# Block transposes on VectorE and piecewise transfers in place of TensorE transposes, in a fused attention and ELU feed-forward kernel

## The chip, the cores and the metric

The kernel runs on one core of a Trainium2 chip. The metric is the device time of one execution in microseconds. The profile adds one traced execution, with the start, the duration and the releaser of every instruction.

## The reference

`x` is (8, 8, 512, 64): batch, head, token, depth. `state` is (8, 8, 32, 64). For each batch and head there are two small attentions, and their results are concatenated along the tokens and reshaped to 4352 rows of 512. These rows go through a feed-forward layer with an ELU between two products.

```python
scores = x @ state.T / 8               # 512 x 32 per head
xread  = softmax(scores) @ state
scores2 = state @ x.T / 8              # 32 x 512 per head
sread  = softmax(scores2) @ x
h   = concat(xread, sread) @ w_in      # 512 -> 2048
out = elu(h) @ w_out                   # 2048 -> 512
```

## The kernel before

**Stages.** The tokens of one batch (512 rows) are one unit of work. Batch 0 is interleaved by hand with the loading and conversion of the weights (`first_batch`, line 706); its written plan also computes the attention of batch 1. Then `batch(b)` (line 814) runs for b = 1 to 7. It has two parts: `ffn1` (line 412), sixteen column blocks `fo` of the first product, each followed by the ELU (`exp_part` on ScalarE, `max_part` on VectorE, into `g_all`); and the second product by Strassen's method (from line 531), where single products are themselves split once more (`Second`, line 472). At the end `states` (line 852) does the rows of the states of all batches.

**The attention of the next batch.** `batch(b)` puts the attention of batch b+1 into its second product. `attention` (line 668) returns a list of functions, `hooks`; after each step of the Strassen product one of them is called (lines 843 to 846). A full product is six half-size pieces p1a, p1b, p2a, p2b, p6a, p6b, and then the split products, in the order 7, 5, 4, 3; in batch 1 only 4 and 3 are split, and products 7 and 5 are two pieces each. Before the change the hooks are: `s0` after p1a, which turns `x` on TensorE (`turn_x`, line 225) into four PSUM banks and copies it out with ScalarE (`copy_x`); `s1` after p1b, with the scores (`scores`, line 261), the combined weights m = state @ w_in (`make_m`, line 377) and the chain of both softmaxes over VectorE, ScalarE and GpSimd; `s2` after p6a, which turns the states' softmax weights `a_s` on TensorE (`turn_state`, line 321), copies them out (`copy_state`, into `aT_s`) and turns the tokens' weights on VectorE (`turn_tokens`, `t_sb` to `aT`); and `state_read` (line 333) after p6b, the product of `aT_s` with `x`.

**Order.** Instructions issued through `InOrder` (line 93) keep the order in which the program calls them as long as `on` is true. For TensorE and for the transfer queue of SyncE it stays true. For VectorE it is true until the end of the `ffn1` loop of batch 1 (line 827) and false afterwards; for ScalarE and GpSimd it is false from batch 1 on. There a scheduler sets the order when the program is built. Since the helper at line 100 records every operation, the profile gives nearly all instructions line 100, and they are told apart by the names of their tiles.

**Buffers.** The pool `o` (line 76) has two buffers; before the change `xT` (the turned `x`) and the two output tiles `o_sb` share it. The pool `work` (tag `w`) has eleven; six of them hold the weight sums `t_w` for good, and five rotate over `s`, `s_2`, `aT_s` and others. `x_sb` has one buffer, so `load_x` of the next batch waits for `state_read`. `w_in` holds half of the first weight at a time: `fetch_w_in(2, 0)` and `fetch_w_in(0, 0)` bring the halves back from a copy in DRAM, two transfers of 1 MB each, on SyncE's queue.

**PSUM.** `ffn1` rotates over banks 3, 4 and 5. A split product accumulates into two banks, called x and y, seven times four matmuls (`Second.run`, line 505): x, y, x, y, x, y, x. After each four, VectorE adds a bank to `o_sb` or ScalarE copies it; the next four that go to the same bank wait for that.

Of the kernel before, what the change touches and what calls it, by code (L numbers as in the profile page):

```python
# [10 lines left out]
FP32 = mybir.dt.float32  # L11
# [14 lines left out]
def kernel(  # L26
# [15 lines left out]
    B, H, S, D = x.shape  # L42
    NS = state.shape[2]
    DM, DF = moe_w_in.shape
    P = 128
    R = S // P
    NP = H // 2
    G = 2
# [16 lines left out]
    def pool(name, bufs, **kw):  # L65
        return ctx.enter_context(tc.tile_pool(name=name, bufs=bufs, **kw))
# [6 lines left out]
    work = pool("work", NRAW + 4)  # L73
    small = pool("small", 4)
    epool = pool("elu", 3)
    opool = pool("o", 2)
# [8 lines left out]
    def bank(i):  # L85
        return psum[:, i]

    def pair(i):

        return psum[:, i : i + 2]  # L90
# [3 lines left out]
    class InOrder:  # L94
# [10 lines left out]
    tensor, sync, vector, scalar, gpsimd = (  # L105
        InOrder(e) for e in (nc.tensor, nc.sync, nc.vector, nc.scalar, nc.gpsimd)
    )
    matmul = tensor.matmul

    def transpose(out, in_):  # L110


        for t in range(2):
            rows = slice(t * 64, (t + 1) * 64)
            tensor.transpose(out[:, t], in_[rows], ident[rows, rows], tile_position=(t * 64, 0))
# [15 lines left out]
    x_t, st, m_t = {}, {}, {}  # L131

    def load_x(b, engines):
        x_t[b] = xpool.tile([P, R, DM], FP32, name="x_sb")
        x_v = x[b].rearrange("h (p r) d -> p r h d", r=R)
        for r in range(R):
            engines[r % len(engines)].dma_start(
                out=x_t[b][:, r].rearrange("p (h d) -> p h d", d=D), in_=x_v[:, r]
            )

    state_v = state.rearrange("b (m c) n d -> c m n b d", c=G)

# [82 lines left out]
    def turn_x(b, i, first=6):  # L225

        ps = pair(first).rearrange("p t (j r q) -> p t j r q", j=2, q=64)
        for j in range(2):
            for r in range(R):
                m = 2 * i + j  # L230
                transpose(ps[:, :, j, r], x_t[b][:, r, m * P : (m + 1) * P])
        st[b, "xT", i] = ps

    def copy_x(b, i):
        xT = opool.tile([P, 2, R * P], FP32, tag="o", name="xT")
        for j in range(2):
            st[b, 2 * i + j] = xT[:, j]
            scalar.copy(
                out=xT[:, j].rearrange("p (r t q) -> p t r q", t=2, q=64),
                in_=st[b, "xT", i][:, :, j],  # L240
            )
# [19 lines left out]
    def scores(b):  # L261

        st[b, "s_ps"] = by_state(b, [st[b, m][:, None] for m in range(NP)])
# [57 lines left out]
    def turn_state(b):  # L321
        ps = st[b, "sT"] = pair(6).rearrange("p g (r q) -> p g r q", r=R)
        for g in range(G):
            a = st[b, g, "a_s"].rearrange("p (r q) -> p r q", r=R)
            for r in range(R):
                tensor.transpose(ps[:, g, r], a[:, r], ident)

    def copy_state(b):
        st[b, "aT_s"] = work.tile([P, G, R, P], FP32, tag="w", name="aT_s")
        for g in range(G):  # L330
            scalar.copy(out=st[b, "aT_s"][:, g], in_=st[b, "sT"][:, g])

    def state_read(b):


        ps = st[b, "sr"] = pair(6)
        for g in range(G):
            for r in range(R):
                for m in range(NP):
                    matmul(  # L340
                        ps[m * NS : (m + 1) * NS, g, :D],
                        st[b, "aT_s"][:, g, r, m * NS : (m + 1) * NS],
                        x_t[b][:, r, m * P + g * D : m * P + (g + 1) * D],
                        start=(r == 0),
                        stop=(r == R - 1),
                        tile_position=(0, m * NS),
                    )

    def keep_read(b):
        for g in range(G):  # L350
            scalar.activation(
                out=read[:, b, g], in_=st[b, "sr"][:, g, :D], func=AF.Copy,
                scale=st[b, g, "total"],
            )
# [14 lines left out]
    def fetch_w_in(c, k):  # L369

        for i in range(2):
            sync.dma_start(
                out=w_in[:, 2 * (k + i) : 2 * (k + i) + 2],
                in_=w_in_mem[:, 2 * (c + i) : 2 * (c + i) + 2],
            )

    def make_m(b, c, h=None, first=6):

        c_in = c if b < 2 else c % 2
        halves = slice(2 * c_in, 2 * c_in + 2) if h is None else slice(2 * c_in + h, 2 * c_in + h + 1)  # L380
        assert h is None or b == 0
        st[b, "m", c] = by_state(b, [w_in[:, halves, m] for m in range(NP)], first)

    def copy_m(b, c, g, copy):
        if g == 0:
            m_t[b, c] = mpool.tile([P, G, 512], FP32, name="m_sb")
        copy(out=m_t[b, c][:, g], in_=st[b, "m", c][:, g])
# [8 lines left out]
    def exp_part(ps):  # L396
        e = epool.tile([P, ps.shape[-1]], FP32, tag="e", name="e_sb")
        scalar.activation(out=e, in_=ps, func=AF.Relu, scale=-1.0)
        scalar.activation(out=e, in_=e, func=AF.Exp, scale=-1.0)
        return e  # L400

    def max_part(fo, e, ps):
        vector.scalar_tensor_tensor(
            out=g_all[:, fo, : ps.shape[-1]], in0=e, scalar=-1.0, in1=ps,
            op0=ALU.add, op1=ALU.max,
        )

    def elu(ps, fo):

        max_part(fo, exp_part(ps), ps)  # L410

    def ffn1(b, fo):


        ps = bank(4 + fo % 2 if b == 0 else 3 + (fo + 1) % 3)
        for k in range(G):
            matmul(
                ps,
                m_t[b, fo // 4][:, k, fo % 4 * P : (fo % 4 + 1) * P],
                st[b, k, "aT"],  # L420
                start=(k == 0),
                stop=(k == G - 1),
            )
        return ps
# [243 lines left out]
    def attention(b):  # L668


        def both(*fs):
            for g in range(G):
                for f in fs:
                    f(b, g)

        def s0():

            for i in range(2):
                turn_x(b, i, 4 + 2 * i)
            for i in range(2):  # L680
                copy_x(b, i)

        def s1():

            scores(b)
            for c in range(2):
                make_m(b, c, first=4 - 2 * c)
            both(column_max, turn_scores, column_exp, row_max, row_subtract, row_exp)
            both(row_sum, row_scale, column_total)
            for c in range(2):  # L690
                for g in range(G):
                    copy_m(b, c, g, (scalar.copy, vector.tensor_copy)[g])

        def s2():
            turn_state(b)
            copy_state(b)
            both(turn_tokens)

        nop = lambda: None
        return [s0, s1, nop, nop, s2, lambda: (state_read(b), keep_read(b))]  # L700

    def store(b, i, o_sb):
        rows = out_b[b, 0:S].rearrange("(p r) c -> p r c", r=R)
# [108 lines left out]
            store(0, i, o_sb)  # L812

    def batch(b):
        for fo in range(FO):
            elu(ffn1(b, fo), fo)
            if fo == FO // 4 + 1:
                for c in (2, 3):
                    make_m(b, c, first=6 if c == 2 else 0)
            if FO // 4 + 1 <= fo < FO // 4 + 5:  # L820
                c, g = divmod(fo - FO // 4 - 1, G)
                copy_m(b, 2 + c, g, vector.tensor_copy)
            if b == 1 and fo % 2 == 1:
                weight_sum((1, 2, 4, 3)[fo // 4], fo % 4 // 2)
            if b > 1 and fo == FO // 4 + 2:
                fetch_w_in(0, 0)
        vector.on = False
        nxt = b + 1 < B
        hooks = attention(b + 1) if nxt else [turn_read]
        if nxt and b > 0:  # L830
            s1 = hooks[1]
            hooks[1] = lambda: (s1(), fetch_w_in(2, 0))
        if b + 2 < B:
            hooks += [lambda: load_x(b + 2, [sync])]
        if b == 1:
            hooks += [lambda: second[4].weights(t_w[4]), lambda: second[3].weights(b22)]
            hooks += [lambda: second[5].weights(t_w[1]), lambda: second[7].weights(t_w[3])]
            used = {k: second[k] for k in (4, 3)}
        else:
            used = second  # L840
        whole = Strassen(2, used)
        whole.sums()
        for f in whole.steps():
            f()
            if hooks:
                hooks.pop(0)()
        if not nxt:
            fetch_w_in(2, 2)
        for i in (1, 0):
            store(b, i, whole.o_sb[i])  # L850
# [28 lines left out]
    for b in range(1, B):  # L879
        batch(b)  # L880
# [31 lines left out]
```

## Time and profile before

| | |
|---|---|
| median of 3 runs | 756.91 us (756.82 to 757.55) |
| profiled span | 756.0 us |
| transposes of `x` on TensorE (64x64, in all) | 256, 11.8 us busy |
| transposes of `a_s` on TensorE (128x128, in all) | 64, 8.4 us busy |
| ScalarE copies `xT`, `aT_s` (all batches) | 16.6 us and 8.6 us busy |

In the table by groups a line gives engine, operation, output and inputs by tile name, shape, count, then busy time, mean duration of one, and the idle time of the engine just before them with what ended it. A timeline line gives start, duration, engine, operation and count. TensorE records two matmuls for each fp32 product and one for each transpose: "128x256 x16" is eight matmuls of the program, "ident,x_sb x32" 32 transposes.

### The profile page before, as it was taken

What the parts mean: (1) busy time and instruction counts of PE and PEld (TensorE: products, weight loads), DVE (VectorE), ACT (ScalarE), POOL (GpSimd) and SP (SyncE); (2) the same over time, 40 slices, a digit from 0 to 9 for tenths busy, and PEclk for the clock granted to TensorE, in tenths of its full rate; (3) what the DMA queues carried; (4) which work ended last, traced back from release to release, by engine and by line L of the source; (5) the groups of instructions that cost most, each with busy time, mean ns of one, the idle gap of its engine ahead of it and who ended that gap; (6) DMA issues with size and microseconds to landing.
All of it is one profiled execution on the core that took longest, in us unless ns stands there. A gap on an engine that the chain in (4) does not pass through costs nothing.

```text
span 756.0 us, 11509 instructions
## 1 busy us (share of the span) xinstructions
PE 736.2 (97%) x4712; PEld 512.6 (68%) x4712; DVE 465.4 (62%) x856; ACT 312.0 (41%) x575; POOL 34.4 (5%) x38
## 2 busy tenths in 40 slices
PE   4899999999999999999999999999999999999997
PEld 2544344368955797468946795479846894699886
DVE  2999974899246673667455763667366755557330
ACT  5899955653036311642055303631164205510420
POOL 0200002002000200011000200020000100000000
PEclk9999999999999999999999999999999999999999
DMA  9667900403212331214030221233121103003000
GB/s 284 212 202 245 310 0 23 91 1 117 51 64 104 112 57 57 111 69 100 29 140 0 113 56 60 108 113 56 57 112 57 56 29 139 1 0 141 28 4 26
DMA packets 49566, 66.81 MB, mean 88 GB/s; under 512 B 36968, under 2 KB 37480, under 8 KB 45672
## 3 DMA queue, kind: packets, MB, share of 16 engines
q1 hardware_dynamic: 47204, 65.45, 26.3%
q10 hardware_dynamic: 2308, 0.62, 0.4%
q8 instruction: 37, 0.61, 0.4%
q14 instruction: 17, 0.14, 0.1%
HBM read 52.95 MB, written 13.11 MB: 87 GB/s over the span
## 4 chain that ended last, share of the span: by engine, by line
PE 93%; DVE 3%; DMA 1%; ACT 1%; ACTq 0%; issue 0%; DVEq 0%
PE ps L100 93%; DVE w_in L100 1%; DMA x_sb<-in_x_dram 1%; DVE s L100 0%; DMA raw<-in_moe_w_out_dram 0%; DVE w_out L100 0%; ACT xT L100 0%; DVE g_all L100 0%; ACTq L100 0%; DVE top L100 0%; ACT raw L100 0%; ACT a_s L100 0%; DVE t_sb L100 0%; ACT e_sb L100 0%; DVE aT L100 0%; DVE m_sb L100 0%
## 5 line engine op out<-in xcount | busy, mean ns | idle before, releaser
L100 PE MATMUL ps<-w_out,g_all 128*128 128x256 f32 (+2 forms) x1088 | 234.8, 367 | 1.5 <-DVE g_all L100 0.8
L100 PE MATMUL ps<-aT,m_sb 128*128 128x512 f32 x512 | 226.3, 595 | 1.1 <-DVE m_sb L100 0.8
L100 PEld LDWEIGHTS ps<-w_out,g_all 128*128 128x128 f32 x1088 | 175.6, 191 | 55.0 <-issue 37.1
L100 PEld LDWEIGHTS ps<-aT,m_sb 128*128 128x128 f32 x512 | 95.4, 190 | 122.0 <-issue 116.9
L100 ACT ACTIVATE e_sb<-ps 128x512 f32<-128x512 f32 (+1 forms) x144 | 82.5, 573 | 218.8 <-PE ps L100 203.5
L100 DVE SCALAR_TENSOR_TENSOR g_all<-e_sb,ps 128x512 f32<-128x512 f32 (+1 forms) x144 | 94.4, 657 | 112.5 <-ACT e_sb L100 112.4
L100 DVE TENSOR_TENSOR o_sb<-o_sb,ps 128x128 f32<-128x128 f32 (+2 forms) x170 | 52.8, 310 | 76.1 <-PE ps L100 74.4
L100 PE MATMUL ps<-t_w,s 128*128 128x256 f32 (+1 forms) x480 | 89.3, 338 | 0.0
L100 ACT ACTIVATE e_sb<-e_sb 128x512 f32<-128x512 f32 (+1 forms) x144 | 87.3, 606 | 4.6
L100 PEld LDWEIGHTS ps<-t_w,s 128*128 128x128 f32 x480 | 77.1, 191 | 7.3 <-DVE o_sb L100 0.2
L100 ACT COPY o_sb<-ps 128x512 f32<-128x512 f32 (+2 forms) x52 | 21.2, 424 | 122.2 <-PE ps L100 115.2
L100 ACT ACTIVATE raw<-raw 128x512 f32<-128x512 uint32 x64 | 43.8, 684 | 1.0
L100 POOL TENSOR_TENSOR t_sb<-t_sb,top_t 128x512 f32<-128x512 f32 x16 | 16.7, 1049 | 533.5 <-DVE top_t L100 533.5
L100 DVE TENSOR_TENSOR s<-s,g_all 128x512 f32<-128x512 f32 (+1 forms) x36 | 32.1, 896 | 14.4 <-PE ps L100 14.2
L100 DVE TENSOR_TENSOR g_all<-g_all,s 128x512 f32<-128x512 f32 (+1 forms) x36 | 31.9, 886 | 9.6 <-PE ps L100 9.6
L100 PE MATMUL ps<-w_in,kT 64*32 64x512 f32 (+1 forms) x576 | 33.2, 547 | 0.8 <-ACT a_s L100 0.8
L100 DVE TENSOR_TENSOR g_all<-g_all 128x512 f32<-128x512 f32 (+1 forms) x36 | 32.2, 895 | 0.5
L100 PE MATMUL ps<-t_w,g_all 128*128 128x128 f32 (+1 forms) x240 | 32.1, 282 | 0.0
L100 DVE TENSOR_TENSOR s<-g_all 128x512 f32<-128x512 f32 (+1 forms) x36 | 31.6, 895 | 0.5
L100 PE MATMUL ps<-w_in,s 128*128 128x128 f32 x240 | 30.7, 275 | 0.0
L100 PEld LDWEIGHTS ps<-t_w,g_all 128*128 128x128 f32 x240 | 29.8, 192 | 0.5
L100 PEld LDWEIGHTS ps<-w_in,s 128*128 128x128 f32 x240 | 28.7, 192 | 0.0
(82 smaller groups left out, 574.8 us busy)
## 6 DMA issues: line engine op xcount, KB each, us to landing
w_in<-w_in_mem SPq DMA_DIRECT2D x26, 1024.0 KB, 5.9
raw<-in_moe_w_in_dram SPq DMA_DIRECT2D x16, 512.0 KB, 4.9
raw<-in_moe_w_out_dram SPq DMA_DIRECT2D x16, 512.0 KB, 4.4
out_dram<-o_sb SPq DMA_DIRECT2D x16, 512.0 KB, 2.6
x_sb<-in_x_dram SPq DMA_DIRECT2D x30, 256.0 KB, 4.5
w_in_mem<-w_in SPq DMA_DIRECT2D x4, 1024.0 KB, 8.6
x_sb<-in_x_dram ACTq DMA_DIRECT2D x2, 256.0 KB, 6.7
s_sb<-in_state_dram SPq DMA_DIRECT2D x8, 56.0 KB, 2.0
```

Of the source, the lines that this page charges most:

```text
L100: ins = getattr(self.engine, name)(*args, **kw)
```

## The change

`turn_x` and `copy_x` are no longer used for batches 2 to 7, nor `turn_state` and `copy_state`; batches 0 and 1 keep them. The purpose is to take these transposes off TensorE.

For `x`, `load_blocks(b + 1)` starts at the head of `batch(b)`. It reads `x` from DRAM a second time, in sixteen transfers of 64 KB; each fills 32 partitions, so that every 32x32 block lies where a transpose inside the blocks gives its part of the transposed tensor. One contiguous piece is 32 floats, 128 bytes. `turn_blocks` then turns 128x512 at a time on VectorE, four times, called after `fo` 12 to 15. For `a_s`, `move_state` turns the blocks first (two VectorE transposes of 128x512 into `a_blocks`) and puts them in place with sixteen transfers of 32 KB inside SBUF, again in pieces of 128 bytes. The hooks are merged: scores, softmax chain and `move_state` all come after p1a, and `state_read` comes two hooks later than before.

```diff
+    def load_blocks(b):
+        for i in range(2):
+            st[b, "blocks", i] = raw = opool.tile([P, 2, R * P], FP32, tag="o", name="x_blocks")
+            for j in range(2):
+                for k in range(4):
+                    x_v = x[b, 2 * (2 * i + j) + k // 2].rearrange(
+                        "(q p r) d -> p r q d", q=P // 32, r=R
+                    )
+                    sync.dma_start(
+                        out=raw[k * 32 : (k + 1) * 32, j].rearrange(
+                            "p (r q d) -> p r q d", r=R, d=32
+                        ),
+                        in_=x_v[:, :, :, k % 2 * 32 : (k % 2 + 1) * 32],
+                    )
+
+    def turn_blocks(b, m):
+        i, j = divmod(m, 2)
+        if j == 0:
+            st[b, "xT", i] = work.tile([P, 2, R * P], FP32, tag="w", name="xT_b")
+        st[b, m] = st[b, "xT", i][:, j]
+        vector.transpose(st[b, m], st[b, "blocks", i][:, j])
...
+    def move_state(b):
+        st[b, "aT_s"] = work.tile([P, G, R, P], FP32, tag="w", name="aT_s")
+        t = work.tile([P, G, S], FP32, tag="w", name="a_blocks")
+        for g in range(G):
+            vector.transpose(t[:, g], st[b, g, "a_s"])
+        t_v = t.rearrange("p g (r q n) -> p g r q n", r=R, n=NS)
+        for m in range(NP):
+            for q in range(P // 32):
+                sync.dma_start(
+                    out=st[b, "aT_s"][q * 32 : (q + 1) * 32, :, :, m * NS : (m + 1) * NS],
+                    in_=t_v[m * 32 : (m + 1) * 32, :, :, q],
+                )
...
-        def s0():
-            for i in range(2):
-                turn_x(b, i, 4 + 2 * i)
-            for i in range(2):
-                copy_x(b, i)
...
         def s2():
-            turn_state(b)
-            copy_state(b)
             both(turn_tokens)
+            move_state(b)
...
-        return [s0, s1, nop, nop, s2, lambda: (state_read(b), keep_read(b))]
+        return [lambda: (s1(), s2()), nop, nop, nop, nop, nop, lambda: (state_read(b), keep_read(b))]
...
     def batch(b):
+        if b + 1 < B:
+            load_blocks(b + 1)
         for fo in range(FO):
             elu(ffn1(b, fo), fo)
+            if fo > 11 and b + 1 < B:
+                turn_blocks(b + 1, fo - 12)
...
         if nxt and b > 0:
-            s1 = hooks[1]
-            hooks[1] = lambda: (s1(), fetch_w_in(2, 0))
+            s1 = hooks[0]
+            hooks[0] = lambda: (s1(), fetch_w_in(2, 0))
```

## The prediction

> **What bounds the kernel now.** I read the page first: busy time and the chain of waits.
>
> ```profile
> PE 736.2 (97%) x4712; PEld 512.6 (68%) x4712; DVE 465.4 (62%) x856; ACT 312.0 (41%) x575; POOL 34.4 (5%) x38
> PE 93%; DVE 3%; DMA 1%; ACT 1%; ACTq 0%; issue 0%; DVEq 0%
> ```
>
> TensorE sets the time nearly everywhere, so work taken off it counts in full unless it then waits. Second, TensorE's timeline through one batch (b = 3, which makes batch 4; batches 2 to 6 repeat with a period of 82.06 us):
>
> ```profile
> 325.10 3.62 PE L100 MATMUL ps<-w_out,g_all 128*128 128x256 f32 x16
> 328.65 1.22 PE L100 MATMUL ps<-ident,x_sb 64*128 64x64 f32 x32
> 329.80 3.72 PE L100 MATMUL ps<-w_out,g_all 128*128 128x256 f32 x16
> 333.45 1.09 PE L100 MATMUL ps<-xT,kT 64*32 64x512 f32 x16
> 334.33 1.92 PE L100 MATMUL ps<-w_in,kT 64*32 64x512 f32 x32
> ...
> 346.65 1.04 PE L100 MATMUL ps<-ident,a_s 128*128 128x128 f32 x8
> 347.52 3.62 PE L100 MATMUL ps<-t_w,s 128*128 128x256 f32 x16
> 351.07 1.10 PE L100 MATMUL ps<-x_sb,aT_s 128*32 128x64 f32 x64
> 352.10 2.05 PE L100 MATMUL ps<-w_out,g_all 128*128 128x128 f32 x16
> 353.99 1.06 PE L100 MATMUL ps<-w_in,s 128*128 128x128 f32 x8
> 355.19 1.16 PE L100 MATMUL ps<-w_out,g_all 128*128 128x128 f32 x8
> ```
>
> Starts matter, since durations overlap. The two ident rows go away. Split product 7 begins at 352.10; from 353.99 to the next row it takes 1.20 us where 0.90 is the pace (677.60 to 678.50 in batch 7). The chain of waits in order of time says why:
>
> ```profile
> 354.17 0.04 DVEq L100
> 354.20 0.73 DVE s L100 x2
> 354.94 0.21 DVE o_sb L100
> 355.14 0.04 issue
> ```
>
> VectorE reached the addition of bank y to `o_sb` late, behind the sums of `s`. The fourth foursome needs that bank. Third, VectorE's timeline in batch 1, which is full there:
>
> ```profile
> 158.17 0.68 DVE L100 SCALAR_TENSOR_TENSOR g_all<-e_sb,ps 128x512 f32<-128x512 f32 x1
> 161.56 0.69 DVE L100 SCALAR_TENSOR_TENSOR g_all<-e_sb,ps 128x512 f32<-128x512 f32 x1 [0.38 <-ACT e_sb L100]
> 169.69 0.69 DVE L100 TENSOR_REDUCE top<-ps 128x1 f32<-128x512 f32 x1 [0.18 <-PE ps L100]
> ```
>
> Its idle time from 143 to 169 us is some 0.6 us. Last, the nearest rows for the new operations:
>
> ```profile
> L100 DVE STREAM_TRANSPOSE aT<-t_sb 128x512 f32<-128x512 f32 x16 | 11.3, 706 | 10.6 <-POOL t_sb L100 10.6
> x_sb<-in_x_dram SPq DMA_DIRECT2D x30, 256.0 KB, 4.5
> s_sb<-in_state_dram SPq DMA_DIRECT2D x8, 56.0 KB, 2.0
> ```
>
> **What the Trainium skill says.** "VectorE: DVE Perf Modes", The three transpose paths: VectorE turns only inside 32x32 blocks. That fits the change's need of transfers; the trace's `aT` transpose takes 0.706 us. "DMA: Bandwidth & Descriptors", Specifications: pieces under 512 bytes do not run at line rate. The trace agrees in part: `x_sb` in pieces of 256 bytes moved at 184 to 271 GB/s (transfer view, 350 to 375 us), stores of `o_sb` at up to 426. Same page, Why small descriptors are slow (HBM only): moves inside SBUF are spared that; no row shows one. "TensorE: Matmul & The Clock Gate", Architectural detail: the array is 16× 32×32, not 1× 128×128: VectorE and ScalarE take their queue strictly in order. The late `o_sb` above agrees.
>
> **The change part by part, steady batches (b = 2 to 6).**
> Removed from TensorE: the Strassen stage with attention takes 52.52 us (571.30 to 623.82); without, in batch 7, 46.83 less 0.65 for the turning of `read`, 46.18. So attention costs 6.34. Scores 0.88, m 1.85 and state read 1.03 stay, 3.76. The difference is 2.58: about 2.07 of transposes with their switching and 0.51 of the stall (352.10 to 356.18 is 4.08; batch 7 takes 3.57).
> ScalarE's copies go: hidden before, no gain.
> Added to VectorE: six transposes at about 0.63 start to start, 3.8 us. In the built order the first four stand after `fo` 4, 5, 9 and 12, earlier than they are called. VectorE idles 1.03 us in most `fo` slots of 1.72, so they fit; behind each stand the next ELUs, for which TensorE would wait, so the blocks must have landed. The store of batch 2's last `o_sb` goes out at 296.1; the sixteen transfers follow. I take 0.5 us each: 0.444 was measured for `s_sb`'s issue (224 pieces, 32 partitions), and `x_sb` moved 4096 pieces in about 4.4 us, 17 ns per piece on each of 16 engines, so 512 pieces need 0.54 us if a piece costs the same. They land at about 301, 303, 305 and 307; VectorE wants them at 306.3, 311, 317 and 322. Even 1.1 us each is in time. `fetch_w_in(0, 0)`, queued behind them, is issued at 307.17 anyway.
> Moved: scores start at 328.65 instead of 333.45. The VectorE chain from `top` (334.72) to the second `aT` took 10.6 us; it now starts at 329.6, with two transposes of `a_s` mostly inside its waits for GpSimd (0.56 and 1.23 us), and ends at 340.7. Three sums for product 7, now behind it, end at 342.5. The subtractions after p2 follow (TensorE done at 341.9). p6 ends at 348.9, the second addition to `s` at 350.2. The built order now has the `o_sb` addition directly after it: ready 350.7, done 351.0, and the fourth foursome needs it at 351.6. So the stall goes.
> New wait: the next `s_2` takes over the buffer of `a_blocks`, and so waits on VectorE's queue for all sixteen transfers of `move_state`. Behind it stands an `o_sb` addition that TensorE needs at 354.3; three other operations first make that 352.2 for the landing. `a_blocks` is full at 339.6; sixteen issues at 0.45 and 2.0 to land give 348.9. Bounds: 0.38 each (the shortest issue of `x_sb`), 347.7; 0.75, 353.8. I take 348.9, 3.3 us to spare. `state_read`, at about 355, needs the same transfers. `fetch_w_in(2, 0)` and `load_x` come later, and are wanted only in the next batch.
> Gain: 5 x 2.58 = 12.9 us.
>
> **Batch 1.** VectorE keeps program order to the end of `ffn1`, and it is full. In the built order three transposes come between the ELUs of `fo` 12 to 15; after the ELU of `fo` 15 (ends 162.2) follow three sums of 1.15 and one of 0.6, and then the fourth transpose: 162.2 + 3.45 + 0.6 + 0.65 = 166.9. TensorE reaches the scores at 163.6, and their second half (0.45 later) wants it: a wait of about 2.8 us that was not there. Against 2.07 saved: 0.8 us lost. Later in the batch VectorE keeps up (the first product 7 piece starts at 186.8, its bank is free at 183.4).
> Sum: 756.9 - 12.9 + 0.8 = 744.8 us.
>
> **The rivals.**
> The stall stays or a like one comes (VectorE has 3.8 us more per batch, and the margins in product 7 are 0.6 us): only 2.07 are gained, 756.9 - 5 x 2.07 + 0.8 = 747.4. For it speaks that VectorE is the releaser of the only stall; against it the built order.
> The moves inside SBUF take 0.75 us each: the `s_2` wait ends 1.6 us late, each batch gains 1.0: 756.9 - 5.0 + 0.8 = 752.7. No row shows such a transfer; `s_sb` speaks against it.
> The small pieces are the new bound, slower: at 1.2 us each `move_state` lands at 361.0, 8.8 late; each batch loses 6.2: 756.9 + 31.0 + 0.8 = 788.7. For it speaks that no piece of 128 bytes is in the trace; against it that 256 pieces in 1.2 us would be 75 ns per piece and engine, four times `x_sb`'s.
> No change: gains and waits cancel, 757.
>
> **How the numbers follow.** 0.67 for 744.8 (with 742 if batch 1 does not wait), 0.13 for 747.4, 0.09 for 752.7, 0.03 for no change, 0.08 for slower. The range goes from 742.0 to 752.0, which takes in the first two and part of the third. Faster 0.88, same 0.03, slower 0.09.
>
> **What would show it.** Right: no ident rows in batches 2 to 6 and a period of 79.5 us; a gap of 2 to 3 us inside the scores of batch 1 with `xT_b` as releaser; no gap in product 7; transfers of `a_blocks` issued at 0.4 to 0.5 us. Wrong: gaps in `ffn1` released by `x_blocks`, gaps in product 7 released by `s` behind transfers, or a shortest period over 80 us.

## The result, and the profile after

The changed kernel takes 747.33 us (median of four executions: 746.17, 746.29, 748.36, 749.0) where the kernel before takes 757.23; the ratio is 0.987, with an interval of 0.9846 to 0.9895. The two longer executions had a mean granted clock of TensorE (as a share of its full clock) of 0.998 and 0.995 in place of 1.0; the profiled one is that of 746.17 us.

The page of the kernel after, busy time and the chain of waits:

```profile
PE 723.7 (97%) x4472; PEld 502.5 (68%) x4472; DVE 486.0 (65%) x892; ACT 293.3 (39%) x539; POOL 34.4 (5%) x38
PE 89%; DVE 6%; SPq 1%; DMA 1%; ACT 1%; issue 1%; POOL 0%; ACTq 0%; DVEq 0%; POOLq 0%
```

TensorE lost 12.5 us of work and 240 records, VectorE gained 20.6 us and 36 instructions, and TensorE still holds the chain, with a little less of it: some percent went over to VectorE and to SyncE's transfer queue.

TensorE's timeline through the same batch as in the prediction (start, duration, engine, operation, tiles, count):

```profile
322.99 3.62 PE L100 MATMUL ps<-w_out,g_all 128*128 128x256 f32 x16
326.54 1.09 PE L100 MATMUL ps<-xT_b,kT 64*32 64x512 f32 x16
327.42 1.92 PE L100 MATMUL ps<-w_in,kT 64*32 64x512 f32 x32
329.28 10.63 PE L100 MATMUL ps<-w_out,g_all 128*128 128x256 f32 x48
...
353.04 1.10 PE L100 MATMUL ps<-x_sb,aT_s 128*32 128x64 f32 x64
354.07 2.05 PE L100 MATMUL ps<-t_w,s 128*128 128x128 f32 x16
356.08 1.16 PE L100 MATMUL ps<-w_in,s 128*128 128x128 f32 x8
```

Both rows with `ident` are gone and the scores follow p1a directly. The stall at the fourth foursome of product 7 is gone too; small ones are left: from 354.07 to 356.08 are 2.01 us where 1.79 is the pace.

Batch 1 on TensorE, and then the VectorE instruction that ended its wait (two timelines of the kernel after; the brackets give the idle time before a row and what ended it):

```profile
159.29 3.62 PE L100 MATMUL ps<-w_out,g_all 128*128 128x256 f32 x16
162.83 1.07 PE L100 MATMUL ps<-xT_b,kT 64*32 64x512 f32 x12
166.23 0.62 PE L100 MATMUL ps<-xT_b,kT 64*32 64x512 f32 x2 [2.32 <-DVE xT_b L100]
...
168.93 10.63 PE L100 MATMUL ps<-w_out,g_all 128*128 128x256 f32 x48
```

```profile
162.61 2.35 DVE L100 TENSOR_TENSOR s<-g_all 128x1024 f32<-128x1024 f32 x2
164.87 0.68 DVE L100 TENSOR_TENSOR t<-t_w,t 128x512 f32<-128x512 f32 x1
165.47 0.70 DVE L100 STREAM_TRANSPOSE xT_b<-x_blocks 128x512 f32<-128x512 f32 x1
```

The scores wait 2.32 us for the fourth transpose, which stands behind the sums for the Strassen product.

Where the time went, by the starts of the first `ffn1` product of each batch (all from TensorE's timelines):

| | before | after | difference |
|---|---|---|---|
| up to batch 1 | 129.50 | 128.72 | -0.78 |
| batch 1 | 83.99 | 85.12 | +1.13 |
| batches 2 to 6 | 410.33 | 398.78 | -11.55 |
| batch 7 and the states | 132.18 | 131.78 | -0.40 |
| span | 756.0 | 744.4 | -11.6 |

The first row is not the change's: nothing is changed ahead of batch 1, and in the nine profiles here in which the clock is full up to there, batch 1 begins at 128.3 to 129.5 us, whatever the kernel. In the last row TensorE's own rows agree to 0.01 us up to its last product; the 0.40 us lie behind it, and their cause is not shown. On TensorE the change gives 11.55 - 1.13 = 10.4 us. The periods of batches 2 to 6 are 79.61, 79.71, 79.53, 79.67 and 80.26 us (82.07 before): not quite the same from batch to batch.

The longest is the one in which a single issue of the sixteen took 1.25 us. Its chain of waits (kernel after, batch 6):

```profile
583.00 1.25 SPq L100
...
586.91 1.90 DMA aT_s<-a_blocks
...
589.14 0.70 DVE s L100
...
591.16 0.21 DVE o_sb L100
...
591.41 2.61 PE ps L100 x74
```

A sum of `s` on VectorE waits for the last transfer, the addition to `o_sb` stands behind it, and a foursome of product 7 on TensorE waits for the addition. The prediction had named such a gap as a sign of being wrong; one batch of five shows it.

### The profile page after: what moved, and what is told of

It is laid out like the page before. It is cut to its first block, busy times and chain, and to the rows that moved or that the text cites. A ratio compares the mean times of both kernels' runs of the same rounds, so it can differ in the third digit from the quotient of the medians.

```text
span 744.4 us, 11377 instructions
## 1 busy us (share of the span) xinstructions
PE 723.7 (97%) x4472; PEld 502.5 (68%) x4472; DVE 486.0 (65%) x892; ACT 293.3 (39%) x539; POOL 34.4 (5%) x38
## 4 chain that ended last, share of the span: by engine, by line
PE 89%; DVE 6%; SPq 1%; DMA 1%; ACT 1%; issue 1%; POOL 0%; ACTq 0%; DVEq 0%; POOLq 0%
PE ps L100 89%; DVE w_in L100 2%; SPq L100 1%; DMA x_sb<-in_x_dram 1%; DVE g_all L100 1%; DVE total_t L100 0%; DVE s L100 0%; DVE top L100 0%; DVE w_out L100 0%; ACT e_sb L100 0%; POOL t_sb L100 0%; ACT xT L100 0%; DVE xT_b L100 0%; DVE aT L100 0%; DVE t_sb L100 0%
## 5 line engine op out<-in xcount | busy, mean ns | idle before, releaser
L100 PEld LDWEIGHTS ps<-w_out,g_all 128*128 128x128 f32 x1088 | 176.6, 191 | 53.5 <-issue 37.1
L100 ACT COPY o_sb<-ps 128x512 f32<-128x512 f32 (+2 forms) x52 | 20.6, 424 | 151.7 <-PE ps L100 144.6
```

The costliest lines, as they stand in the source:

```text
L100: ins = getattr(self.engine, name)(*args, **kw)
```

## The experiments

All run beside the kernel before, which took 757.3 to 757.4 us in each group. Where an edit is given against the changed kernel, the diff says so by its context.

### The changed kernel again

No edit.

> The changed kernel once more, to see how its runs spread. In its trace TensorE stands idle for 2.3 us inside the scores of batch 1, and two of its four runs were 2.2 and 2.8 us longer, with a mean granted clock of 0.998 and 0.995. Theory A (the long idle time lets the clock drop in some executions): runs near 746.2 and near 748.5, the longer ones at a clock below 1. Theory B (chance): all near 746.2.

Measured: 748.37 us (746.37, 748.29, 748.45, 748.65), ratio 0.9878 (0.9863 to 0.9893). The profiled execution, 746.37 us, has batch 1 in 85.13 us and the gap of 2.32 us. So over eight executions there are two groups: 746.2 to 746.4 with a mean clock of 1.0 (three), and 748.3 to 749.0 with 0.998 or 0.995 (five).

### Earlier transposes of x

```diff
-            if fo > 11 and b + 1 < B:
-                turn_blocks(b + 1, fo - 12)
+            if 7 < fo < 12 and b + 1 < B:
+                turn_blocks(b + 1, fo - 8)
```

Only in batch 1, where VectorE keeps the order of the program, does this move anything.

> The changed kernel with turn_blocks called after fo 8 to 11 instead of 12 to 15. The built order changes in batch 1 alone, where the fourth transpose no longer stands behind the sums. Theory A (the wait of batch 1 costs 2.8 us and triggers the lower clock): batch 1 takes 51.8 us instead of 54.6, the median falls to about 743.5, all runs at clock 1. Theory B (VectorE is full in batch 1 and the wait only moves to another instruction): batch 1 stays within 0.5 us of 54.6 and the time at 746 to 748.

Measured: 747.09 us (746.77 to 747.58), ratio 0.9867 (0.9853 to 0.9882). TensorE's timeline of batch 1 in this kernel:

```profile
159.22 1.99 PE L100 MATMUL ps<-aT,m_sb 128*128 128x512 f32 x4 [0.34 <-DVE g_all L100]
161.04 3.62 PE L100 MATMUL ps<-w_out,g_all 128*128 128x256 f32 x16
164.58 1.09 PE L100 MATMUL ps<-xT_b,kT 64*32 64x512 f32 x16
...
190.62 1.05 PE L100 MATMUL ps<-x_sb,aT_s 128*32 128x64 f32 x58 [1.42 <-DMA aT_s<-a_blocks]
```

The gap in the scores is gone, but `ffn1` now waits for the ELUs (31.71 us from the head of the batch to p1a, 30.57 before the edit), and the state read waits 1.42 us for the transfers. From p1a on, the stretch for which the expectation had 51.8 or about 54.6 us, batch 1 takes 53.5, but `ffn1` takes up what is won there: as a whole it takes 85.25 us, against 85.12. Moving the transposes moves the wait; what is lost in batch 1 is room on VectorE.

### A filler in the gap of batch 1

Six products `ident` by `ident` into bank 1, whose result nothing uses, ahead of the scores of batch 2.

```diff
+    FILL = 6
...
+            if b == 2:
+                for i in range(FILL):
+                    matmul(bank(1)[:, :P], ident, ident, start=True, stop=True)
             scores(b)
```

> The changed kernel with six products of the identity with itself into an unused bank ahead of the scores of batch 2; they fill about 2 us of the time in which TensorE waits there. No result uses them. Theory A (it is the idle time that lowers the clock): the time stays at 746.2 within 0.5, and no run is at a clock below 1. Theory B (the longer runs have another cause): longer runs near 748.5 still occur, about as often as without.

Measured: 748.03 us (747.67 to 749.96), ratio 0.9878 (0.9861 to 0.9894). The wait in the scores is 0.98 us in place of 2.32, and batch 1 is as long as before the edit, 85.13 us. The profiled execution is the longest of the four, at a mean clock of 0.997; its clock fell at 25 to 30 us of the span (0.66 there), in batch 0, and not in batch 1. Theory A's 746.2 us was missed: the three executions at full clock took 747.7 to 748.3 us. Late transfers are a likely part of that: in the profile single issues of the last two batches took 1.62 and 1.77 us, and the five periods make 400.28 us where the changed kernel has 398.78. On its own this run says little on the clock; it is taken up below.

### The states' part alone

x goes through TensorE again (`s0`, `copy_x`); `move_state` stays, and the softmax chain and the turning of the tokens come one hook after `s0`.

```diff
-        return [lambda: (s1(), s2()), nop, nop, nop, nop, nop, lambda: (state_read(b), keep_read(b))]
+        return [s0, lambda: (s1(), s2()), nop, nop, nop, nop, lambda: (state_read(b), keep_read(b))]
...
-        if b + 1 < B:
-            load_blocks(b + 1)
...
-            if fo > 11 and b + 1 < B:
-                turn_blocks(b + 1, fo - 12)
```

> Only the states' part of the change: x is turned on TensorE after p1a and copied by ScalarE as before, the scores stand after p1b again, and the softmax weights are turned on VectorE and moved by the sixteen transfers. The chain then starts 5 us later: a_blocks is full at 344.5 on the clock of the kernel before, sixteen issues at 0.655 us and 1.9 to land give 356.9, while the sums of product 5 want the buffer at 352.8. Theory A (the wait for the transfers on VectorE's queue counts as soon as they are late): product 7 loses about 3.5 us in each of five batches against 1.4 gained, near 767. Theory B (VectorE has room, the wait costs nothing): five times 1.4 and 0.9 gained, near 749.

Measured: 758.21 us (median of 20 executions), ratio 1.0014 (1.0007 to 1.002): neither of the expected times. The steady period is 81.55 us, 0.5 below before, and batch 1 takes 87.27 us, 3.3 more than before. TensorE's timeline in batch 1 of this kernel:

```profile
190.53 1.89 PE L100 MATMUL ps<-x_sb,aT_s 128*32 128x64 f32 x58 [2.35 <-DMA aT_s<-a_blocks]
192.34 4.29 PE L100 MATMUL ps<-w_out,g_all 128*128 128x256 f32 x16
```

The state read waits 2.35 us for the transfers, and the products after the wait are slow: 1.89 us where 1.10 is usual for the whole row, 4.29 where 3.72 is. The granted clock from 190 to 200 us is 0.83, so some 1.7 of the 3.3 us are the clock. In the steady batches the sixteen transfers are issued from 346.37 on for 10.40 us; the last is issued at about 356.2 and lands some 1.9 us later, at 358.1, less than a microsecond before the state read at 358.99. So the transfers are in time there. But VectorE's sums, which come later here, hold up two foursomes of product 7: these start 1.10 and 1.14 us after the ones before them (at 354.87 and 357.90), where 0.89 is the pace. What five batches still gain, batch 1 takes back.

### The part on x alone

```diff
         def s2():
+            turn_state(b)
+            copy_state(b)
             both(turn_tokens)
-            move_state(b)
...
-        return [lambda: (s1(), s2()), nop, nop, nop, nop, nop, lambda: (state_read(b), keep_read(b))]
+        return [s1, nop, nop, nop, s2, lambda: (state_read(b), keep_read(b))]
```

> Only the part on x: blocks and VectorE's transposes for x of batches 2 to 7; the states' weights are turned by TensorE again, where they were. Theory A, the parts are additive: state_only's shortest period (81.55 us from batch to batch) is 0.51 below before's 82.06, and the whole change gains 2.45, so x alone must gain 1.94 a batch, a period of 80.1; with batch 1 losing about 1.1 as in the whole change (the gap of 2.3 us in its scores must be there, released by xT_b) the time is 756.9 - 9.7 + 1.1 = 748.3 us. Theory B, each part gains only its own products and the stall of product 7 goes only with both: 1.15 a batch for x, period 80.9, 756.9 - 5.8 + 1.1 = 752.2. Records of a clock of 0.998 or 0.995 in about half of the executions (the gap of 2.3 us is there), which makes them 2 us longer.

Measured: 753.75 us (753.59 to 754.47), ratio 0.9952 (0.9937 to 0.9967). The period is 80.72 us in each of the steady batches that the profile shows, a gain of 1.35, close to theory B's 1.15. Product 7 on TensorE in batch 3 of this kernel:

```profile
354.31 1.06 PE L100 MATMUL ps<-w_in,s 128*128 128x128 f32 x8
355.51 1.16 PE L100 MATMUL ps<-w_out,g_all 128*128 128x128 f32 x8
```

From 354.31 to 355.51 are 1.20 us: the stall of the kernel before, to the hundredth. So the two parts are not additive. x alone gives 1.35 a batch and the states alone 0.5; together they give 2.36 to 2.54, and 1.8 in the batch with the slow issue. VectorE's rows show why the stall stays; first x alone, then the same place in the changed kernel:

```profile
349.78 1.23 DVE L100 TENSOR_TENSOR s<-s,g_all 128x1024 f32<-128x1024 f32 x1 [4.10 <-PE ps L100]
...
354.57 0.69 DVE L100 TENSOR_TENSOR s<-s 128x512 f32<-128x512 f32 x1
355.18 0.28 DVE L100 TENSOR_TENSOR o_sb<-o_sb,ps 128x128 f32<-128x128 f32 x1
```

```profile
346.85 1.23 DVE L100 TENSOR_TENSOR s<-s,g_all 128x1024 f32<-128x1024 f32 x1 [0.50 <-PE ps L100]
348.70 0.29 DVE L100 TENSOR_TENSOR o_sb<-o_sb,ps 128x128 f32<-128x128 f32 x1 [0.63 <-PE ps L100]
```

With x alone VectorE is not late: it stood idle for 4.10 us ahead of the two sums that wait for p6. But four more sums of `s` stand between these and the addition to `o_sb`, as in the kernel before (352.44 to 354.86 us there); in the changed kernel there is none. So the stall is a matter of the order that was built for VectorE. The order with the addition first came with the states' part: the states alone have it too, only with later sums. Why the scheduler built another order is not shown. Batch 1 took 87.70 us in the profile, 3.7 more than before, with the gap of 2.33 us for `xT_b`, and a clock of 0.84 from 160 to 170 us.

### Twice the transfers for the states

```diff
-                sync.dma_start(
-                    out=st[b, "aT_s"][q * 32 : (q + 1) * 32, :, :, m * NS : (m + 1) * NS],
-                    in_=t_v[m * 32 : (m + 1) * 32, :, :, q],
-                )
+                for g in range(G):
+                    sync.dma_start(
+                        out=st[b, "aT_s"][q * 32 : (q + 1) * 32, g, :, m * NS : (m + 1) * NS],
+                        in_=t_v[m * 32 : (m + 1) * 32, g, :, q],
+                    )
```

> The whole change, but move_state makes 32 transfers of half the size (one for each half g of the heads) in place of 16; the bytes and the 128-byte pieces are the same. Theory A, an issue costs 0.65 us whatever it holds: 32 take 20.8 us, a_blocks lands at 337.5 + 20.8 + 1.9 = 360.2 on batch 3's clock where TensorE's state read wants it at 353.0, so each of the five steady batches loses about 7 us: 746.3 + 35 = 781 us, and batch 1 some more. Theory B, an issue costs by its pieces: 0.33 us each, the landing stays and the time is 746 to 748.

Measured: 795.46 us, ratio 1.0501 (1.048 to 1.0522). SyncE's queue and then TensorE in batch 3 of this kernel:

```profile
356.38 20.61 SPq L100 DMA_DIRECT2D aT_s<-a_blocks  x32
```

```profile
377.71 2.17 PE L100 MATMUL ps<-x_sb,aT_s 128*32 128x64 f32 x58 [4.52 <-DMA aT_s<-a_blocks]
379.81 2.62 PE L100 MATMUL ps<-t_w,s 128*128 128x128 f32 x16
```

An issue takes 20.61 / 32 = 0.64 us for 128 pieces, as much as for 256. Among these transfers the price is one of the transfer, not of its bytes or pieces. Batches 2 to 6 take 436.34 us (225.88 to 662.22), 37.6 more than in the changed kernel, where theory A expected 35. Batch 1 takes 94.76 us, 9.6 more, where "some more" had been said, and batch 1 began 2.4 us later; this and the 37.6 make the 49.6 us between the two spans. Part of the loss is again a slow clock after a wait (0.75 from 378 to 384 us; 2.62 us where 2.05 is usual): around the end of each of the five steady batches' waits, of 4.5 to 5.3 us, the granted clock is 0.50 for 3.4 or 6.8 us.

### Two queues for the states' transfers

```diff
-                sync.dma_start(
+                (sync, scalar)[q % 2].dma_start(
                     out=st[b, "aT_s"][q * 32 : (q + 1) * 32, :, :, m * NS : (m + 1) * NS],
```

> The whole change, but every other one of move_state's sixteen transfers is issued by ScalarE's queue. Theory A, the price is the issue (0.65 us on one queue, whatever the pieces) and the late landing costs the last batch 0.6 us and more at times: the landing comes about 5 us earlier, the last period (80.26 us) falls to 79.6, and the undisturbed time from 746.3 to 745.6. Theory B, the landing costs nothing: 746.3 and the same periods. Theory C, the transfers themselves are the price (they share the 16 DMA engines): the landing comes at the same time, 10.7 + 1.9 us after a_blocks is full.

Measured: 747.24 us (746.7, 747.2, 747.29, 748.63), ratio 0.9868 (0.985 to 0.9886). The two queues in batch 3 of this kernel, from the timelines of SyncE and of ScalarE:

```profile
339.75 5.50 SPq L100 DMA_DIRECT2D aT_s<-a_blocks  x8
```

```profile
339.72 5.23 ACTq L100 DMA_DIRECT2D aT_s<-a_blocks  x8
```

They issue side by side, at 0.69 and 0.65 us each, about as before, and the landing takes the same 1.9 us (median): it is over about 5 us earlier. TensorE then runs without its small waits (1.89 us between these two rows, 2.01 in the changed kernel):

```profile
356.23 2.05 PE L100 MATMUL ps<-t_w,s 128*128 128x128 f32 x16
358.12 1.13 PE L100 MATMUL ps<-w_in,s 128*128 128x128 f32 x8
```

All five periods are 79.50 or 79.51 us, the last one too. This is theory A for the batches 2 to 6, worth 1.25 us in sum (398.78 to 397.53). The scheduler also put a sum of `s` ahead of an addition to `o_sb` in this kernel. That the landing and not the order is what counts is shown by the batches of the five kernels that turn both and use one queue (the change twice, the earlier transposes, the filler, and batch 1 left as before), 25 in all. What a batch loses against 79.51 us follows the end of its last issue, counted from the start of p1a: 0.02 to 0.16 us where that is at 25.0 us, 0.20 to 0.54 at 25.3 to 25.4, 0.75 to 0.79 at 25.6 to 25.8, and 1.16 to 1.26 at 26.0 to 26.1. In the three kernels with two queues it is at 20.1 to 21.3 us, and none of the 15 batches loses anything, not even the one in which an issue took 1.92 us.

The time did not fall to 745.6 because batch 1 took 86.83 us in place of 85.12. TensorE there, in this kernel:

```profile
166.84 0.62 PE L100 MATMUL ps<-xT_b,kT 64*32 64x512 f32 x2 [2.32 <-DVE xT_b L100]
...
167.31 4.00 PE L100 MATMUL ps<-w_in,kT 64*32 64x512 f32 x26
```

and in the changed kernel's profile, the row that answers to the last:

```profile
166.70 2.30 PE L100 MATMUL ps<-w_in,kT 64*32 64x512 f32 x26
```

The same 26 records take 4.00 us and 2.30 us: after the same wait the clock was lower in one of the two executions. Two windows of this kernel, and below them two of the changed kernel (length, busy time of TensorE, its weight loads, VectorE, ScalarE and GpSimd, then the granted clock, the DMA share and GB/s):

```profile
163.97:167.38 3.41, 1.09 (x28) 0.27 (x24) 3.41 (x5) 0.00 (x0) 0.00 (x0) 1.00 0.00 0
167.38:170.79 3.41, 3.41 (x36) 0.72 (x20) 3.01 (x7) 0.79 (x2) 0.00 (x0) 0.50 0.02 5
```

```profile
162.09:165.50 3.41, 1.82 (x16) 0.55 (x14) 3.41 (x5) 0.00 (x0) 0.00 (x0) 1.00 0.00 0
165.50:168.92 3.42, 2.69 (x36) 0.73 (x36) 3.39 (x7) 0.75 (x2) 0.00 (x0) 1.00 0.02 5
```

Half the clock for 3.41 us is 1.7 us, the whole difference of batch 1. The Trainium skill has this in "TensorE: Matmul & The Clock Gate", What's actually happening: half the clock after an idle window of about 3.4 us, the window running freely, so that it depends on the moment. The traces agree on the length and on the free running: in all twelve the clock changes only at whole multiples of 3.41 us from the start of its record, and the windows above are cut at these multiples. They differ on how idle the window has to be. TensorE was busy for 1.09 of the 3.41 us before the fall; where the same wait of 2.32 us lies across two windows, busy for 1.82 and 2.69 us, the clock stays. In the twelve traces 16 such windows at full clock have TensorE busy for less than 1.5 us, and half the clock followed 15 of them; of the more than 2500 others it followed one.

### Batch 1 left as before

x and states of batch 2, whose turning lies in batch 1, go through TensorE; batches 3 to 7 as in the change.

```diff
         def s2():
+            if b == 2:
+                turn_state(b)
+                copy_state(b)
             both(turn_tokens)
-            move_state(b)
+            if b > 2:
+                move_state(b)
...
+        if b == 2:
+            return [s0, s1, nop, nop, s2, read_state]
...
-        if b + 1 < B:
+        if 1 < b < B - 1:
             load_blocks(b + 1)
```

> Batch 2's x and states (whose work lies in batch 1) are turned by TensorE as before; batches 3 to 7 as in the whole change. Theory A, VectorE, full in batch 1, is what the change loses there: batch 1 takes 83.99 us as before and not 85.12, and the periods stay 79.5 to 79.7; the undisturbed execution is 746.3 - 1.1 = 745.2. Clock: if the lower mean clock of 0.998 in five of eight executions of the whole change comes with the 2.3 us for which TensorE waits in batch 1, no execution here shows 0.998 or 0.995 (0.997, which before shows too, may come), and the median is 745.2 to 745.6. Rival, the clock falls for another reason and batch 1's loss is elsewhere: 746.3 undisturbed, median 747 to 748.

Measured: 746.83 us (745.99, 746.46, 747.21, 747.28), ratio 0.9858 (0.9843 to 0.9872). Batch 1 takes 83.99 us, exactly as before, so the 1.13 us are the change's. But the transfers were late in more of the other batches than they were in the changed kernel's profile: periods of 79.64, 79.53, 80.27, 80.67 and 80.04 us. Product 7 of batch 5 in this kernel:

```profile
509.41 1.06 PE L100 MATMUL ps<-w_in,g_all 128*128 128x128 f32 x8
511.21 1.16 PE L100 MATMUL ps<-w_out,g_all 128*128 128x128 f32 x8 [0.74 <-DVE o_sb L100]
```

There one of the sixteen issues took 1.61 us in place of 0.61, and `s`, behind the transfers on VectorE, held up the `o_sb` addition. So the time was missed: the two executions at full clock took 745.99 and 746.46 us, not 745.2. The expectation on the clock failed too: two of four executions have a mean clock of 0.998, though in the profile TensorE's longest wait in batch 1 is 0.76 us.

### Both remedies together, and the filler with two queues

The first joins the two edits above; the second adds the six unused products of the filler to the kernel with two queues.

> keep_b1 and two_queues together: batch 2 turned by TensorE as before, batches 3 to 7 as in the change, move_state's transfers issued by two queues. Theory A (batch 1's loss is VectorE being full and the clock that falls after its wait; the rest of the loss is the landing of sixteen transfers from one queue): batch 1 takes 83.99 us as before, all five periods 79.51 as in two_queues, so the span is that of keep_b1's profile less the 2.6 us by which its five periods exceed 5 x 79.51: 744.3 - 2.6 = 741.7, a time of 743.5 us, with executions within 0.5 us of each other. Rival, the two don't add because the late landings of keep_b1 come from its own order of VectorE's work: 745 to 746.5.

Measured: 745.09 us (744.43, 744.63, 745.09, 745.58, 746.09), ratio 0.9834 (0.9821 to 0.9848). In the profile batch 1 takes 83.99 us and all five periods are 79.51. The profiled execution, the longest, had its clock down in batch 0 (0.68 from 20 to 30 us) and reached batch 1 at 130.59 us, 2.3 later than the kernel with batch 1 left as before did; its span of 743.9 less that is 741.6, the 741.7 expected. The periods and batch 1 are theory A's; the time is not: 743.5 us with executions within 0.5 us of each other was expected, and the fastest took 744.43 us, the slowest 1.7 more. Executions without a trace leave open where the rest went. It has the lowest median of the kernels here, though its interval overlaps those of batch 1 left as before and of the next kernel.

> two_queues with the six unused products of filler in front of the scores of batch 2, in bank 1; the rest is the same. Theory A, TensorE's clock falls for some 10 us after a wait of 2.3 us, and this is what the lower mean clock of 0.998 means: the wait is cut to 1.0 us, so no profile or execution has the 0.87 of 160 to 170 us that two_queues has there; batch 1 takes 85.1 us and not 86.83, the periods stay 79.51, and the time is 747.2 - 1.7 = 745.5 us, 745.0 without the clock's fall at the start (0.997). Rival, the fall of the clock doesn't depend on this wait: 747 us as two_queues, with 0.998 and 0.995 among the executions.

Measured: 746.19 us (744.67, 745.91, 746.47, 747.65), ratio 0.9851 (0.9834 to 0.9867), between theory A's 745.5 and the rival's 747. The profiled execution takes 744.67 us, with batch 1 in 85.13 us, periods of 79.51, and the clock at 1.00 throughout; TensorE in its batch 1:

```profile
162.44 1.50 PE L101 MATMUL ps<-ident 128*128 128x128 f32 x12
...
165.93 0.62 PE L101 MATMUL ps<-xT_b,kT 64*32 64x512 f32 x2 [0.98 <-DVE xT_b L101]
```

One of its four executions still has 0.998, and another 747.65 us at 0.999, for which there is no trace. So on the clock: with the wait of 2.3 us in the scores (the change twice, x alone, two queues) two of the four profiles have the clock down at 160 to 180 us, and 12 of the 16 executions a mean of 0.998 or 0.995; without it (earlier transposes, the two fillers, the two that leave batch 1 alone) none of the five profiles has it down there, and 4 of the 21 executions have such a mean, as have 3 of 39 of the kernel before. In the four profiles the work in a window tells which: in the two that fell, x alone and two queues, TensorE was busy for 1.09 us of one window, in the other two for no less than 1.82 of any. The mean alone doesn't tell where the clock fell: the profile of two queues has 0.997, which 17 of the 39 of the kernel before have too. In two kernels without the wait the profile shows a fall at the start of the kernel instead, again after windows with little work (1.38 us busy in the filler, 1.45 in both remedies together; 1.96 in the kernel before, which kept its clock). Where the executions without a trace lost theirs stays open.

## Why the prediction was right, and where it was off

**The sum.** Predicted were 744.8 us, with a range of 742.0 to 752.0, and the likeliest case held: the time lay in the range, 2.5 us above the figure. Executions at full clock took 746.2 to 746.4 us, 1.5 above it. The rest, about 1 us of the median, is the clock, which the prediction did not price.

**TensorE's transposes and the stall: right.** 2.58 us a batch were predicted, and a period of 79.5. With the transfers in time the period is 79.51 (two queues), a gain of 2.56. The stall went by the last step that the prediction names, the addition to `o_sb` directly behind the second addition to `s` in the built order. That step was right; an earlier chain on VectorE is not enough, since x alone has it and keeps the old order and the 1.20 us.

**The transfers' issue: mis-sized.** The step took 0.45 us for each of `move_state`'s issues and 0.5 for `x_blocks`, from the 0.444 of `s_sb`. In the trace they take 0.61 and 0.64 us (0.65 and 0.68 from one to the next), and twice as many of half the size take 0.60 each: the idea that an issue is paid by the piece was wrong. The trace of before held a warning, the issues of `x_sb` (shortest, median and longest, in ns), of which the prediction used the shortest alone:

```profile
L100 SPq DMA_DIRECT2D x_sb<-in_x_dram x30: 383/636/1864, 1.5 to 518.0; - x30
```

`a_blocks` was full 14.5 us after p1a began, exactly as predicted (339.6 - 325.1, and 337.5 - 323.0), and the landing took 1.9 us against 2.0. So the landing came at 349.6 - 323.0 = 26.6 us in place of 23.8, and the 3.3 us to spare shrank to about half a microsecond. The deadline itself, 27.1 us after p1a, was less than a microsecond too late as well: at 26.6 us a batch lost 0.2, and at 26.9 (batch 6, with one slow issue) 0.75. In sum that took 1.25 us of the 12.9. The rival with 0.75 us an issue, at 752.7, was nearer on the issue, 0.65, than the 0.45 taken; its time was further off. `x_blocks` landed from 297 to 308 us and `ffn1` never waited for it, as predicted. The prediction's landing sums are 0.1 to 0.2 us off (339.6 + 16 x 0.45 + 2.0 is 348.8); nothing rests on that.

**Batch 1: right in kind, too small.** A wait in the scores was predicted, released by the fourth transpose at 166.9. It came at 166.2, which is 167.0 on the clock of before, since batch 1 began 0.78 us earlier in this profile. The trace calls 2.32 us idle where about 2.8 were predicted, and yet 1.13 us were lost against 0.8. The step that was off is the 0.45 us of scores that were to run ahead of the wait and so to shorten it. In the kernel before, TensorE's scores and m in batch 1 are these:

```profile
168.41 1.09 PE L100 MATMUL ps<-xT,kT 64*32 64x512 f32 x16
...
171.15 7.17 PE L100 MATMUL ps<-w_out,g_all 128*128 128x256 f32 x32
```

All of them took 2.74 us (168.41 to 171.15). In the changed kernel what is left of them after the wait takes 2.70 us (166.23 to 168.93), though 12 of the 16 records of the scores had run before it: these saved nothing. So the whole time from 162.83 to 166.23 is lost, 3.4 us; less the 2.07 for the transposes that makes 1.3, near the 1.13. That VectorE is full there was right, as the earlier transposes showed: the wait only moved. What the prediction put at nothing is what comes after a wait, a slower clock in some executions, 1.7 us at a time. The wait that it foresaw was shorter than the window of 3.4 us, and the trace of before, in which the clock is 1.0 throughout, shows no such fall.

**The rivals.** "The stall stays or a like one comes" (747.4) hits the median, but by chance: the profile shows neither five stalls nor a period of 80.0, but 1.25 us from late transfers, 0.3 more from batch 1 and about 1 us of clock. The small pieces as the new bound (788.7) did not come about; with twice the transfers, at 795 us, the moves did become the bound, by their number and not by their pieces.

## What to carry to other kernels

A re-layout by many small transfers is paid by the issue: count the transfers, multiply by the measured price of one on its queue, and see whether the last lands before the first instruction that waits for it; two queues halve that. Take the stage in which the receiving engine is full out of the change: here one batch of six, kept as it was, gave back 1.13 us in the profile. And when a change opens a wait on TensorE, look at how the wait lies in the steps of 3.41 us in which the clock changes: here it cost 1.7 us more where it left TensorE busy for only 1.09 us of one step.

## What the runs showed of the hardware

- The issue of a transfer with 32 partitions in pieces of 128 bytes takes 0.60 to 0.64 us (median) on SyncE's queue, whether it has 128, 256 or 512 pieces, and on ScalarE's queue 0.62 for 256, with both issuing at once. Other shapes differ: 0.44 for `s_sb`, also with 32 partitions, and 0.38 to 1.86 for `x_sb`. What sets the price stays open. The Trainium skill says in "DMA: Bandwidth & Descriptors", Issuing engines are not separate DMA queues, that several issuing engines save only the time on the sequencer, usually small beside the transfer. The first half agrees; here that time, 16 x 0.65 = 10.4 us, was five times the 1.9 us in which a transfer of 32 KB lands.
- Single issues took 1.25 and 1.61 us, and their landing 3.2 and 3.6 us. Sixteen in a row on one queue, with about half a microsecond to spare, cost 0.75 us or more in 7 of 25 batches.
- After a wait of 2.3 us TensorE ran slower in some executions: 4.00 us for products that otherwise take 2.30. The granted clock changed only in steps of 3.41 us, between 1.00 and 0.50. After 15 of 16 steps with less than 1.5 us of work it was 0.50; a step with 1.82 us of work kept it. With waits of 4.5 to 5.3 us in each steady batch (twice the transfers) the mean clock of the whole execution was 0.972 to 0.974.
- Score records that ran ahead of a wait saved nothing: the last 4 of 16 and m took 2.70 us after it, where all of them took 2.74 in one go.
